# Quartered state products, decoding behind the eviction and tables on another queue in a retention and two-layer kernel

## The chip, the cores and the metric

The kernel runs on one core of a Trainium2 chip. The metric is the device time of one execution in microseconds; before the change it is 597.9 us, the median of three runs (597.83 to 599.41).

## What is computed

Three stages, each on the output of the one before, 1536 tokens in all (2 sequences of 768), 512 features:

```python
def _attn_ref(q, k, v):                      # q, k, v: (2, 8, 768, 64)
    for t in range(S):
        state = gamma[None, :, None, None] * state + np.einsum('bhd,bhe->bhde', k[:, :, t], v[:, :, t])
        y[:, :, t] = scale * np.einsum('bhd,bhde->bhe', q[:, :, t], state)

def _moe_ref(x, w_in, w_out):                # (512, 2048), (2048, 512)
    h = x @ w_in
    g = h * np.tanh(softplus(h))
    return g @ w_out

def _moe2_ref(x, w_gate, w_val, w_out):      # (512, 1536) twice, (1536, 512)
    gate = 1.0 / (1.0 + np.exp(-(x @ w_gate)))
    return gate * (x @ w_val) @ w_out
```

## The kernel before

**Attention.** The tokens are cut into 12 blocks of 128, six to a sequence. A block's queries and keys come as `qk` (128 x 2 x 4 x 128: a pair of heads on the two halves of the partitions, four pairs), its keys and values by token as `nv`. `at_scores(j)` makes the scores of the eight heads in two PSUM tiles, one for each half of the partitions; VectorE multiplies them with a mask into `a`. `at_state(j)` adds the block's keys times values to a running state in PSUM, which ScalarE copies to `s`. `at_out(j)` makes the block's output in one PSUM tile `ao`: eight products of `a` with the decayed values `vp`, and, where the sequence has earlier blocks, eight products of the state with the queries (`inter`). These last have 64 rows and 64 columns, so each uses a quarter of the array; before the change they use the two quarters on its diagonal. VectorE evicts `ao` times a decay table `og` into the chunk `acc` (four blocks each). GpSimd makes `vp` and `og` (`at_prep`).

**Two layers.** Every product of the layers is made of three on rounded numbers (`mm3`): operand and weight are both split into a high part (ScalarE, `fp32r`) and a low part (VectorE or GpSimd, value minus high part). Weights arrive as 64-bit words and are decoded to 32-bit ones first: one ScalarE operation (L100) and three on VectorE (L101 to L103, `decode`). The operands of the first chunk are `xc`; those of the other two chunks are `B11`, `B21`, `B22` and the combinations `T1` to `T4`, which save products. `load_piece` asks for a raw weight, `pump` decodes the next one (a step of `steps`), `put` notes its high and low part in `late_hi` and `late_lo`, `flush_hi` and `flush` issue them, and `weight` hands a weight to a product.

**Order.** While `early` is set, each engine gets its instructions in the order in which the code is written (`InOrder`); such instructions all bear L66. `blocks(j0, dense, made)` writes that order for four attention blocks: scores of the next block, `pump`, `fin` (state, output, eviction), preparation and loads, and one step of the dense products, so that layer 1 starts on finished chunks beside the attention: chunk 0 with blocks 4 to 7, chunk 1 with blocks 8 to 11 (8 dense products in all, one to a block, each of twelve instructions, `h`). After the last block `early` is cleared, and a scheduler orders the rest: `out1_first` (the first output products, `o`), `plain1`, `pair1`, and so on through both layers. DMAs are issued by SyncE; the four tables (`ck`, `ma`, `og`, `sg`) behind the first block's operands.

Of the kernel before, what the change touches and what calls it, by code (L numbers as in the profile page):

```python
# [9 lines left out]
F32 = mybir.dt.float32  # L10
# [4 lines left out]
ALU = mybir.AluOpType  # L15
PSUM = bass.MemoryType.PSUM

P = 128
# [4 lines left out]
def kernel(ctx, tc, qk, nv, w1i, w1o, w2g, w2v, w2o, ma_in, og_in, sg_in, ck_in, out):  # L23
# [14 lines left out]
    NP = KK  # L38
    D = P // 2
# [4 lines left out]
    SPC = N // P  # L44
    SPB = NSUB // 2
    RING = 10
    STG = 3
    WARM = 6
    AHEAD = 4

    early = [True]
# [20 lines left out]
    pe, dve, act, pool, sync = [InOrder(e) for e in (nc.tensor, nc.vector, nc.scalar, nc.gpsimd, nc.sync)]  # L72
# [8 lines left out]
    ps_o = ctx.enter_context(tc.tile_pool(name="ps_o", bufs=2, space=PSUM))  # L81
# [5 lines left out]
    acc_t = [big.tile([P, KK, N], F32, name=f"acc{c}") for c in range(NCH)]  # L87
# [36 lines left out]
    src = {"w1i": w1i, "w1o": w1o, "w2g": w2g, "w2v": w2v, "w2o": w2o}  # L124
    raws, w_t, owner, dead = [], {}, [], set()
    cnt = {"dma": 0, "raw": 0, "task": 0}
    steps, late_hi, late_lo, sums_t, vs = [], [], [], {}, {}
    lo_eng = {"w": dve, "g": pool}

    def load_piece():  # L130
        n = cnt["dma"]
        if n >= len(pieces) or n >= cnt["raw"] + STG:
            return
        kind, i = pieces[n]
        t = stg.tile([P, DM], I64, tag="raw", name="raw")
        sync.dma_start(out=t, in_=src[kind][i])
        raws.append(t)
        cnt["dma"] += 1
# [10 lines left out]
    def room():  # L149
        n = len(owner)  # L150
        return n < RING or owner[n - RING] in dead

    def slot(key):
        assert room(), (key, owner[len(owner) - RING])
        owner.append(key)
        w_t[key] = ring.tile([P, 2, DM], F32R, tag="w", name="w")
        return w_t[key]

    def put(key, v):
        t = slot(key)  # L160
        hi, lo = t[:, 0], t[:, 1]
        late_hi.append(lambda: act.activation(out=hi, in_=v, func=AF.Copy))  # L162
        late_lo.append(lambda: lo_eng["w"].tensor_tensor(out=lo, in0=v, in1=hi.bitcast(F32), op=ALU.subtract))  # L163
        if not early:
            flush()
# [37 lines left out]
    def flush_hi():  # L203
        while late_hi:
            late_hi.pop(0)()

    def flush():
        flush_hi()
        while late_lo:
            late_lo.pop(0)()  # L210

    def pump(n=1):
        flush()
        for _ in range(n):
            if not steps and not plan():
                return
            if steps[0][0] and not room() or steps[0][0] == 0 and "dcs" not in lo_eng:
                return
            steps.pop(0)[1]()

    def weight(key):
        while key not in w_t:
            if not steps:
                assert plan(), key
            steps.pop(0)[1]()
        flush()
        return w_t[key]


# [211 lines left out]
    def run(*parts):  # L441
        for p in parts:
            for s in p:
                s()


    with ExitStack() as actx:
# [4 lines left out]
        ma = ac.tile([P, 1, P], F32, name="ma")  # L452
        ck = ac.tile([P, SPB, 2 * NP, 1], F32, name="ck")
        sg = ac.tile([P, SPB, NP, 1], F32, name="sg")
        og0 = ac.tile([P, NP, P], F32, name="og0")
        qk_t, nv_t, a_t, vp_t, og_t, st_t, s_t = {}, {}, {}, {}, {}, {}, {}

        def load(j):
            if j < NSUB:
                qk_t[j] = ld.tile([P, 2, NP, P], F32, tag="qk", name="qk_t")  # L460
                sync.dma_start(out=qk_t[j], in_=qk[j])
                nv_t[j] = ld.tile([P, 2, 2 * NP, D], F32, tag="nv", name="nv_t")
                sync.dma_start(out=nv_t[j], in_=nv[j])
                if j == 0:
                    sync.dma_start(out=ck, in_=ck_in)
                    sync.dma_start(out=ma, in_=ma_in)
                    sync.dma_start(out=og0, in_=og_in)
                    sync.dma_start(out=sg, in_=sg_in)

        def at_prep(j):  # L470
            if j >= NSUB:
# [21 lines left out]

        def at_out(j):
            a, v, t, s = a_t.pop(j), vp_t[j], qk_t[j], s_t.get(j)
            o = ps_o.tile([P, NP, P], F32, tag="o", name="ao")
            inter = j % SPB > 0

            for p in range(NP):
                for e in range(2):  # L500
                    pe.matmul(
                        out=o[D * e:D * e + D, p, :], lhsT=v[:, 2 * p + e, :], rhs=a[:, e, p, :],
                        start=p == 0, stop=p == NP - 1 and not inter, skip_group_check=True,
                    )
            if inter:
                for p in range(NP):
                    for e in range(2):
                        r = slice(D * e, D * e + D)
                        pe.matmul(
                            out=o[r, p, :], lhsT=s[r, p, :], rhs=t[r, 0, p, :], start=False, stop=p == NP - 1,  # L510
                            skip_group_check=True,
                        )
            dve.tensor_tensor(
                out=acc_t[j // SPC][:, :, j % SPC * P:j % SPC * P + P], in0=o, in1=og_t[j], op=ALU.mult
            )

        def at_state(j):
            if j % SPB == SPB - 1:
                return
            v, k = vp_t[j], nv_t[j]  # L520
            if j % SPB == 0:
                st_t[0] = ps_s.tile([P, NP, D], F32, tag="s", name="st")
            st = st_t[0]
            for p in range(NP):
                for e in range(2):
                    pe.matmul(
                        out=st[D * e:D * e + D, p, :], lhsT=k[:, 0, 2 * p + e, :], rhs=v[:, 2 * p + e, :],
                        start=j % SPB == 0 and p == 0, stop=p == NP - 1, skip_group_check=True,
                    )
            s_t[j + 1] = at.tile([P, NP, D], F32, tag="s", name="s")  # L530
            act.activation(out=s_t[j + 1], in_=st, func=AF.Copy)

        def fin(j):
            at_state(j)
            at_out(j)

        def blocks(j0, dense, made):

            for j in range(j0, j0 + SPC):
                if j + 1 < NSUB:  # L540
                    at_scores(j + 1)
                if j >= SPC - 1:
                    pump()
                fin(j)
                flush_hi()
                at_prep(j + 2)
                load(j + AHEAD)
                load_piece()
                if j == j0 + SPC - 1:
                    made()  # L550
                if dense:
                    dense.pop(0)()
            run(dense)

        dve.memset(ap=one_t, constant=1.0)
        act.activation(out=sig, in_=one_t, func=AF.Mish)
        z = at.tile([P, NP * D], F32, tag="s", name="z")
        dve.memset(ap=z, constant=0.0)
        for n in range(WARM):
            o = ps_o.tile([P, NP * D], F32, tag="o", name="warm")  # L560
# [111 lines left out]
```

## Time and profile before

| | |
|---|---|
| median of the runs | 597.9 us |
| profiled execution, with what lies around it | 602.11 us |
| its span | 600.3 us |
| mean granted TensorE clock | 0.991 |
| TensorE matmul, busy | 587.0 us (98%) |
| VectorE, busy | 412.8 us (69%) |
| GpSimd, busy | 331.3 us (55%) |
| ScalarE, busy | 249.6 us (42%) |

The profile is that of one execution. A program's matrix product in plain fp32 is two instructions in the trace (eight products show as x16), one in `fp32r` is one. In a timeline row stand the start, the length of the merged group, engine, line, operation, the tile written and those read, the shape, the count, and in brackets how long the engine was idle before it and what ended that. PE is TensorE, PEld its weight loads, DVE VectorE, ACT ScalarE, POOL GpSimd.

### The profile page before, as it was taken

What the parts mean: (1) busy time and instruction counts of PE and PEld (TensorE: products, weight loads), DVE (VectorE), ACT (ScalarE), POOL (GpSimd) and SP (SyncE); (2) the same over time, 40 slices, a digit from 0 to 9 for tenths busy, and PEclk for the clock granted to TensorE, in tenths of its full rate; (3) what the DMA queues carried; (4) which work ended last, traced back from release to release, by engine and by line L of the source; (5) the groups of instructions that cost most, each with busy time, mean ns of one, the idle gap of its engine ahead of it and who ended that gap; (6) DMA issues with size and microseconds to landing.
All of it is one profiled execution on the core that took longest, in us unless ns stands there. A gap on an engine that the chain in (4) does not pass through costs nothing.

```text
span 600.3 us, 7975 instructions
## 1 busy us (share of the span) xinstructions
PE 587.0 (98%) x3056; PEld 479.6 (80%) x3056; DVE 412.8 (69%) x572; ACT 249.6 (42%) x433; POOL 331.3 (55%) x268
## 2 busy tenths in 40 slices
PE   9899999999999999998999999999999999999997
PEld 7678887888787888886788787888888888888885
DVE  3879997337959395665777977686578587482554
ACT  1334556445454354443344645642343443333210
POOL 3444566529785585484633556854566657557100
PEclk9989999999999999998999999999999999999999
DMA  8974332204223121401220021133022032000014
GB/s 340 406 252 151 106 106 70 72 3 138 70 72 105 36 84 57 140 23 48 71 70 1 1 106 54 52 105 106 0 88 103 22 101 93 17 1 2 0 53 159
DMA packets 15591, 52.27 MB, mean 87 GB/s; under 512 B 1984, under 2 KB 2112, under 8 KB 15552
## 3 DMA queue, kind: packets, MB, share of 16 engines
q1 hardware_dynamic: 15552, 51.75, 24.9%
q8 instruction: 24, 0.39, 0.3%
q14 instruction: 15, 0.12, 0.1%
HBM read 48.60 MB, written 3.15 MB: 86 GB/s over the span
## 4 chain that ended last, share of the span: by engine, by line
PE 75%; DVE 16%; POOL 3%; ACT 3%; issue 2%; DMA 1%; SPq 0%; DVEq 0%; ACTq 0%; POOLq 0%
PE o L109 30%; PE h L109 28%; PE hx L109 7%; PE h L66 4%; DVE v L102 4%; PE ao L66 3%; DVE v L103 2%; DVE v L101 2%; DVE acc L362 2%; PE sc L66 2%; POOL w L163 1%; POOL g L91 1%; PE st L66 1%; DVE T L91 1%; DMA qk_t<-qk 1%
## 5 line engine op out<-in xcount | busy, mean ns | idle before, releaser
L91 POOL TENSOR_TENSOR g<-e,g 128x512 fp32r<-128x512 f32 x73 | 116.7, 1608 | 86.0 <-ACT g L90 86.0
L109 PE MATMUL o<-g,w 128*128 128x512 f32 x576 | 141.8, 394 | 2.8 <-DVE acc L362 2.6
L109 PEld LDWEIGHTS o<-g,w 128*128 128x128 f32 x576 | 108.6, 190 | 28.3 <-DVE acc L362 5.0
L163 POOL TENSOR_TENSOR w<-v,w 128x512 fp32r<-128x512 f32 x56 | 76.2, 1370 | 67.8 <-ACT w L162 67.0
L109 PE MATMUL h<-T,w 128*128 128x512 f32 x444 | 112.6, 390 | 1.0 <-DVE T L91 0.6
L109 PE MATMUL o<-w,g 128*128 128x512 f32 x432 | 106.0, 390 | 0.0
L109 PEld LDWEIGHTS h<-T,w 128*128 128x128 f32 x444 | 83.2, 188 | 19.4 <-DVE T L91 1.0
L109 PEld LDWEIGHTS o<-w,g 128*128 128x128 f32 x432 | 81.0, 188 | 17.2 <-POOL g L91 0.4
L109 PE MATMUL h<-B,w 128*128 128x512 f32 x348 | 90.8, 390 | 0.8 <-DVE e L352 0.8
L109 PEld LDWEIGHTS h<-B,w 128*128 128x128 f32 x348 | 65.1, 188 | 15.1 <-DVE e L352 1.3
L362 DVE TENSOR_TENSOR acc<-o,acc 128x512 f32<-128x512 f32 x72 | 49.0, 685 | 39.1 <-PE o L109 38.8
L90 ACT ACTIVATE g<-e 128x512 fp32r<-128x512 f32 x77 | 48.1, 630 | 53.7 <-DVE e L352 35.5
L163 POOL TENSOR_TENSOR w<-s,w 128x512 fp32r<-128x512 f32 x34 | 48.2, 1427 | 34.4 <-ACT w L162 34.2
L101 DVE TENSOR_SCALAR v<-v 128x512 int32<-128x512 int32 x59 | 45.1, 767 | 28.1 <-ACT v L100 27.8
L162 ACT ACTIVATE w<-v 128x512 fp32r<-128x512 f32 x59 | 36.7, 630 | 63.1 <-DVE v L103 35.2
L382 DVE TENSOR_TENSOR acc<-o,acc 128x512 f32<-128x512 f32 x60 | 41.1, 686 | 30.6 <-PE o L109 30.2
L100 ACT ACTIVATE v<-raw 128x512 f32<-128x512 f32 x59 | 39.3, 669 | 52.9 <-POOL w L163 20.0
L102 DVE SCALAR_TENSOR_TENSOR v<-raw,v 128x512 int32<-128x512 int32 x59 | 56.0, 951 | 1.0
L109 PE MATMUL hx<-xc,w 128*128 128x512 f32 x216 | 55.6, 390 | 0.1
L103 DVE SCALAR_TENSOR_TENSOR v<-raw,v 128x512 int32<-128x512 int32 x59 | 55.0, 933 | 0.5
L109 PE MATMUL h<-xc,w 128*128 128x512 f32 x216 | 55.0, 389 | 0.0
L109 PEld LDWEIGHTS hx<-xc,w 128*128 128x128 f32 x216 | 40.5, 188 | 8.9 <-ACT e L346 0.5
(78 smaller groups left out, 610.4 us busy)
## 6 DMA issues: line engine op xcount, KB each, us to landing
raw<-w1i SPq DMA_DIRECT2D x16, 512.0 KB, 3.6
raw<-w1o SPq DMA_DIRECT2D x16, 512.0 KB, 3.4
qk_t<-qk SPq DMA_DIRECT2D x12, 512.0 KB, 6.3
nv_t<-nv SPq DMA_DIRECT2D x12, 512.0 KB, 6.8
raw<-w2g SPq DMA_DIRECT2D x12, 512.0 KB, 3.4
raw<-w2v SPq DMA_DIRECT2D x12, 512.0 KB, 3.3
raw<-w2o SPq DMA_DIRECT2D x12, 512.0 KB, 3.2
out<-acc SPq DMA_DIRECT2D x12, 256.0 KB, 2.0
```

Source lines behind the costliest of these rows:

```text
L66: i = call(**kw)
L90: act.activation(out=hi, in_=raw, func=AF.Copy)
L91: eng.tensor_tensor(out=lo, in0=raw, in1=hi.bitcast(F32), op=ALU.subtract)
L100: act.activation(out=v, in_=high.bitcast(F32), func=AF.Copy, scale=2.0 ** -112)
L101: dve.tensor_scalar(out=b, in0=b, scalar1=3, scalar2=None, op0=ALU.logical_shift_left)
L102: dve.scalar_tensor_tensor(out=b, in0=low, scalar=29, in1=b, op0=ALU.logical_shift_right, op1=ALU.bitwise_or)
L103: dve.scalar_tensor_tensor(out=b, in0=high, scalar=SIGN, in1=b, op0=ALU.bitwise_and, op1=ALU.bitwise_or)
L109: pe.matmul(out=o, lhsT=w(a), rhs=x(b), start=first and n == 0, stop=last and n == 2, skip_group_check=more)
L162: late_hi.append(lambda: act.activation(out=hi, in_=v, func=AF.Copy))
L163: late_lo.append(lambda: lo_eng["w"].tensor_tensor(out=lo, in0=v, in1=hi.bitcast(F32), op=ALU.subtract))
L362: dve.tensor_tensor(out=acc, in0=o, in1=acc, op=ALU.add)
L382: dve.tensor_tensor(out=acc, in0=o, in1=acc, op=ALU.add)
```

## The change

Four edits. (1) Odd pairs of heads have their two heads swapped on the partitions, and the output lies in two PSUM tiles, one for even and one for odd pairs, so that the state products use all four quarters of the array; the eviction is two operations of half the size. (2) From the fifth block on, `pump` stands behind the block's eviction instead of ahead of it, and `weight` flushes only if its weight is still pending. (3) Low parts are flushed ahead of `fin`, and at the end of four blocks ahead of the chunk's operands (`made`). (4) ScalarE issues the four table transfers, ahead of everything else on it. One warm-up product goes.

```diff
-    WARM = 6
+    WARM = 5
...
     def weight(key):
...
-        flush()
+        if key in pending:
+            flush()
...
         def load(j):
...
-                if j == 0:
-                    sync.dma_start(out=ck, in_=ck_in)
-                    sync.dma_start(out=ma, in_=ma_in)
-                    sync.dma_start(out=og0, in_=og_in)
-                    sync.dma_start(out=sg, in_=sg_in)
...
         def at_out(j):
-            o = ps_o.tile([P, NP, P], F32, tag="o", name="ao")
+            o = [ps_o.tile([P, NP // 2, P], F32, tag="o", name="ao") for _ in range(2)]
...
             for p in range(NP):
                 for e in range(2):
                     pe.matmul(
-                        out=o[D * e:D * e + D, p, :], lhsT=v[:, 2 * p + e, :], rhs=a[:, e, p, :],
-                        start=p == 0, stop=p == NP - 1 and not inter, skip_group_check=True,
+                        out=o[p % 2][D * e:D * e + D, p // 2, :], lhsT=v[:, 2 * p + e, :], rhs=a[:, e ^ p % 2, p, :],
+                        start=p < 2, stop=p >= NP - 2 and not inter, skip_group_check=True,
...
-                        r = slice(D * e, D * e + D)
+                        r = slice(D * (e ^ p % 2), D * (e ^ p % 2) + D)
                         pe.matmul(
-                            out=o[r, p, :], lhsT=s[r, p, :], rhs=t[r, 0, p, :], start=False, stop=p == NP - 1,
-                            skip_group_check=True,
+                            out=o[p % 2][D * e:D * e + D, p // 2, :], lhsT=s[r, p, :], rhs=t[r, 0, p, :],
+                            start=False, stop=p >= NP - 2, skip_group_check=True,
                         )
-            dve.tensor_tensor(
-                out=acc_t[j // SPC][:, :, j % SPC * P:j % SPC * P + P], in0=o, in1=og_t[j], op=ALU.mult
-            )
+            for n in range(2):
+                dve.tensor_tensor(
+                    out=acc_t[j // SPC][:, n::2, j % SPC * P:j % SPC * P + P], in0=o[n], in1=og_t[j][:, n::2],
+                    op=ALU.mult,
+                )
...
         def blocks(j0, dense, made):
             for j in range(j0, j0 + SPC):
                 if j + 1 < NSUB:
                     at_scores(j + 1)
-                if j >= SPC - 1:
+                flush()
+                if j == SPC - 1:
                     pump()
                 fin(j)
-                flush_hi()
                 at_prep(j + 2)
                 load(j + AHEAD)
                 load_piece()
                 if j == j0 + SPC - 1:
+                    flush()
                     made()
+                if j >= SPC:
+                    pump()
                 if dense:
                     dense.pop(0)()
+                flush_hi()
             run(dense)

+        for t, table in ((ck, ck_in), (ma, ma_in), (og0, og_in), (sg, sg_in)):
+            act.dma_start(out=t, in_=table)
```

(`at_state` and the host's layout of queries and keys swap the same halves of odd pairs; `put` notes each key in `pending`, and `flush` clears it.)

VectorE around the end of the fourth block, before (`v` is a decoded weight, `w` its low part, `ao` the block's output, `xc` the low parts of the first chunk, `a` masked scores):

```order
L66 TENSOR_TENSOR a<-sc,ma 128x512 x2
L66 TENSOR_SCALAR v<-v 128x512
L66 SCALAR_TENSOR_TENSOR v<-raw,v 128x512 x2
L66 TENSOR_TENSOR acc_87<-ao,og 128x4x128
L66 TENSOR_TENSOR xc<-acc_87,xc 128x512 x4
L66 TENSOR_TENSOR a<-sc,ma 128x512 x2
L66 TENSOR_TENSOR w<-v,w 128x512
L66 TENSOR_SCALAR v<-v 128x512
L66 SCALAR_TENSOR_TENSOR v<-raw,v 128x512 x2
L66 TENSOR_TENSOR acc_88<-ao,og 128x4x128
L66 TENSOR_TENSOR w<-v,w 128x512
```

and after:

```order
L66 TENSOR_TENSOR a<-sc,ma 128x512 x2
L66 TENSOR_SCALAR v<-v 128x512
L66 SCALAR_TENSOR_TENSOR v<-raw,v 128x512 x2
L66 TENSOR_TENSOR acc_87<-ao,og 128x2x128 x2
L66 TENSOR_TENSOR w<-v,w 128x512
L66 TENSOR_TENSOR xc<-acc_87,xc 128x512 x4
L66 TENSOR_TENSOR a<-sc,ma 128x512 x2
L66 TENSOR_TENSOR acc_88<-ao,og 128x2x128 x2
L66 TENSOR_SCALAR v<-v 128x512
L66 SCALAR_TENSOR_TENSOR v<-raw,v 128x512 x2
L66 TENSOR_TENSOR a<-sc,ma 128x512 x2
L66 TENSOR_TENSOR w<-v,w 128x512
```

The first weight's low part moved from behind the next score tiles to ahead of the four `xc` parts; the second decoding moved from ahead of the fifth block's eviction to behind it, and its low part behind two more score tiles.

VectorE at the end of the attention, from the low part of the seventh weight after the first, after the change (`acc_89` is the third chunk; the two halves here are the eviction of its third block):

```order
L66 TENSOR_TENSOR w<-v,w 128x512
L101 TENSOR_SCALAR v<-v 128x512
L66 TENSOR_TENSOR acc_89<-ao,og 128x2x128
L102 SCALAR_TENSOR_TENSOR v<-raw,v 128x512
L101 TENSOR_SCALAR v<-v 128x512
L66 TENSOR_TENSOR acc_89<-ao,og 128x2x128
L66 TENSOR_SCALAR v<-v 128x512
L103 SCALAR_TENSOR_TENSOR v<-raw,v 128x512
L102 SCALAR_TENSOR_TENSOR v<-raw,v 128x512
L66 SCALAR_TENSOR_TENSOR v<-raw,v 128x512
```

Two more fused operations, three low parts, one half of the last block's eviction, a scalar operation, the other half, a fused operation, two differences `t`, a fused operation and the first low part of `T` follow. Before, the last block's eviction stood behind one decoding and the first steps of two more, with no low part between.

TensorE at the same place, before and after (`B_84` and `B_85` are `B11` and `B21`, `o` the first output products, `T` the operands made from the third chunk):

```order
L66 MATMUL ao<-a,vp 64x128 x8
L66 MATMUL ao<-qk_t,s 64x128 x8
L109 MATMUL h<-B_84,w 128x512 x6
L109 MATMUL h<-B_85,w 128x512 x6
L109 MATMUL o<-g,w 128x512 x24
L109 MATMUL hx<-T_958,w 128x512
L109 MATMUL h<-T_958,w 128x512 x2
L109 MATMUL o<-g,w 128x512 x12
```

```order
L109 MATMUL h<-B_84,w 128x512 x6
L109 MATMUL h<-B_85,w 128x512 x2
L66 MATMUL ao<-a,vp 64x128 x2
L109 MATMUL h<-B_85,w 128x512 x3
L66 MATMUL ao<-a,vp 64x128 x6
L66 MATMUL ao<-qk_t,s 64x128 x8
L109 MATMUL h<-B_85,w 128x512
L109 MATMUL o<-g,w 128x512 x24
L109 MATMUL hx<-T_980,w 128x512
L109 MATMUL h<-T_980,w 128x512 x2
L109 MATMUL h<-xc,w 128x512 x8
```

The last block's output moved behind eight instructions of the last dense product, and eight `xc` products of a later step stand between the `T` products.

## Rows read from the trace of the kernel before

**Rows 1.** The page, busy us of each engine:
```profile
PE 587.0 (98%) x3056; PEld 479.6 (80%) x3056; DVE 412.8 (69%) x572; ACT 249.6 (42%) x433; POOL 331.3 (55%) x268
```

**Rows 2.** Stretches: length, busy us (count) of the engines, granted clock, DMA share, GB/s:
```profile
27.80:34.60 6.80, 5.99 (x22) 4.57 (x24) 3.77 (x7) 1.92 (x4) 0.00 (x0) 0.50 0.83 321
270.00:280.00 10.00, 7.71 (x28) 5.85 (x27) 5.64 (x9) 2.45 (x4) 3.78 (x3) 0.83 0.20 77
```

**Rows 3.** Timeline of TensorE, first and second dense product:
```profile
28.61 4.63 PE L66 MATMUL h<-xc,w 128*128 128x512 f32 x10 [2.62 <-DVE w L66]
33.18 1.82 PE L66 MATMUL sc<-qk_t 64*128 64x128 f32 x16
...
36.98 3.04 PE L66 MATMUL h<-xc,w 128*128 128x512 f32 x12
```

**Rows 4.** Timeline of TensorE, where the orders meet, and the later wait:
```profile
251.53 2.88 PE L109 MATMUL o<-g,w 128*128 128x512 f32 x12
...
273.02 2.51 PE L109 MATMUL o<-g,w 128*128 128x512 f32 x6 [2.29 <-DVE acc L362]
```

**Rows 5.** Timeline of TensorE, one block with a dense product:
```profile
49.08 3.01 PE L66 MATMUL h<-xc,w 128*128 128x512 f32 x12
52.02 1.16 PE L66 MATMUL sc<-qk_t 64*128 64x128 f32 x16
...
54.60 1.09 PE L66 MATMUL ao<-qk_t,s 64*64 64x128 f32 x16
55.63 3.01 PE L66 MATMUL h<-B,w 128*128 128x512 f32 x12
```

**Rows 6.** Timeline of VectorE beside the first wait:
```profile
20.45 0.42 DVE L66 TENSOR_SCALAR v<-v 128x512 int32<-128x512 int32 x1
20.90 1.42 DVE L66 SCALAR_TENSOR_TENSOR v<-raw,v 128x512 int32<-128x512 int32 x2
22.23 0.68 DVE L66 TENSOR_TENSOR acc<-ao,og 128x512 f32<-128x512 f32 x1
23.61 3.14 DVE L66 TENSOR_TENSOR xc<-acc,xc 128x512 fp32r<-128x512 f32 x4 [0.70 <-ACT xc L66]
26.68 1.27 DVE L66 TENSOR_TENSOR a<-sc,ma 128x512 f32<-128x512 f32 x2
27.88 0.67 DVE L66 TENSOR_TENSOR w<-v,w 128x512 fp32r<-128x512 f32 x1
```

**Rows 7.** Timeline of ScalarE there:
```profile
19.67 0.70 ACT L66 ACTIVATE v<-raw 128x512 f32<-128x512 f32 x1 [2.96 <-DMA raw<-w1i]
...
22.35 0.63 ACT L66 ACTIVATE w<-v 128x512 fp32r<-128x512 f32 x1 [1.71 <-DVE v L66]
...
25.60 0.38 ACT L66 ACTIVATE s<-st 128x256 f32<-128x256 f32 x1
```

**Rows 8.** Stretches, in the order PE, PEld, DVE, ACT, POOL:
```profile
20.00:30.00 10.00, 7.38 (x99) 5.90 (x96) 9.17 (x15) 4.27 (x9) 3.86 (x4) 0.89 1.03 408
40.00:70.00 30.00, 30.00 (x359) 24.55 (x359) 28.53 (x38) 14.82 (x29) 16.90 (x13) 1.00 0.46 159
77.00:251.50 174.50, 173.91 (x761) 142.20 (x760) 120.92 (x163) 84.91 (x149) 112.38 (x81) 1.00 0.25 81
```

**Rows 9.** Timeline of VectorE while GpSimd runs too:
```profile
36.24 1.25 DVE L66 TENSOR_SCALAR v<-v 128x512 int32<-128x512 int32 x1
37.53 2.14 DVE L66 SCALAR_TENSOR_TENSOR v<-raw,v 128x512 int32<-128x512 int32 x2
...
60.73 1.57 DVE L66 TENSOR_TENSOR w<-v,w 128x512 fp32r<-128x512 f32 x1
```

**Rows 10.** Timeline of GpSimd beside the first wait:
```profile
23.36 1.04 POOL L66 TENSOR_TENSOR og<-og,sg 128x512 f32<-128x512 f32 x1
```

**Rows 11.** Timeline of TensorE's weight loads, one block's state products:
```profile
13.42 0.85 PEld L66 LDWEIGHTS ao<-qk_t,s 64*64 64x64 f32 x16 [0.17 <-issue]
```

**Rows 12.** Timeline of TensorE, scores of the second block:
```profile
8.26 1.16 PE L66 MATMUL sc<-qk_t 64*128 64x128 f32 x16 [0.16 <-DMA qk_t<-qk]
```

More of the change, by code (lines that the diff above doesn't have):

```diff
@@ L126 @@
     cnt = {"dma": 0, "raw": 0, "task": 0}
-    steps, late_hi, late_lo, sums_t, vs = [], [], [], {}, {}
+    steps, late_hi, late_lo, pending, sums_t, vs = [], [], [], [], {}, {}
     lo_eng = {"w": dve, "g": pool}
@@ L161, in put @@
         hi, lo = t[:, 0], t[:, 1]
+        pending.append(key)
         late_hi.append(lambda: act.activation(out=hi, in_=v, func=AF.Copy))
@@ L210, in flush @@
             late_lo.pop(0)()
+        pending.clear()
     def pump(n=1):
@@ L525, in at_state @@
                 for e in range(2):
+                    r = e ^ p % 2
                     pe.matmul(
-                        out=st[D * e:D * e + D, p, :], lhsT=k[:, 0, 2 * p + e, :], rhs=v[:, 2 * p + e, :],
+                        out=st[D * r:D * r + D, p, :], lhsT=k[:, 0, 2 * p + e, :], rhs=v[:, 2 * p + e, :],
                         start=j % SPB == 0 and p == 0, stop=p == NP - 1, skip_group_check=True,
@@ L641, in feature_major @@
     def feature_major(a):
-        a = a.reshape(B, H // 2, 2, nsub, P, D).transpose(0, 3, 2, 5, 1, 4)
+        a = a.reshape(B, H // 2, 2, nsub, P, D)
+        a = np.stack([a[:, p, ::1 - p % 2 * 2] for p in range(H // 2)], axis=1).transpose(0, 3, 2, 5, 1, 4)
         return a.reshape(B * nsub, 2 * D, H // 2, P)
```

## The prediction

> **What bounds the kernel now.** I read the page's busy shares first: TensorE works 587.0 of 600.3 us [rows 1], so only what shortens its work, or fills its 13 us of idleness, can count. Next the stretches with the granted clock: it was 0.50, the 1.2 GHz level, from 27.8 to 34.6 us, and fell again in the 270s [rows 2]; each fall follows an idle time of TensorE, 2.62 us and 2.29 us [rows 3, 4]. The third view is TensorE's timeline. The first dense product waits until 28.61 us for a weight's low part on VectorE; its last ten instructions then take 33.18 - 28.61 = 4.57 us, and the scores behind them 1.82 us where they take 1.16 at full clock [rows 3, 5]. From there to the end of the attention TensorE never pauses, and a block with a dense product takes 55.63 - 49.08 = 6.55 us [rows 5]. The fourth view, VectorE and ScalarE beside the first wait, says why it is so long: VectorE does four xc low parts (23.61 to 26.7), then two masked score tiles (26.68), and only then the weight's low part (27.88), though ScalarE had its high part ready at 22.98 [rows 6, 7].
>
> The sum is made against the profiled execution (span 600.3, 602.1 us with what lies around it). The median of the runs is 597.9, 4.2 us below; I carry that difference over unchanged.
>
> **Part 1: low part ahead of operands.** Up to the first decoding I keep the times of before, since they hang on a transfer: ScalarE waits 2.96 us for the raw weight [rows 7] while the DMA engines move 408 GB/s at a share of 1.03 [rows 8], and no byte is added or taken away. Decoding again ends at 22.23 [rows 6]. The eviction is now two halves. No row shows one on VectorE; it lies between 0.34 us (half of 0.68 [rows 6]) and 0.68. ScalarE's 256-column copy takes 0.38 against 0.63 for 512 [rows 7], which is nearest, so 2 x 0.38, and the end at 23.0. Then the weight's low part: 0.67 alone, 1.57 beside GpSimd [rows 6, 9]; GpSimd runs an og multiplication until 24.40 [rows 10], so I take 1.3, and 24.3. The four xc low parts follow at 0.60 each (the first bore 1.3 of their 3.14 us before, beside that og) to 26.7, and TensorE consumes them as they come, three products of 0.245 us ((52.02 - 49.08) / 12 [rows 5]) each. The product ends at about 27.5; before it ended at 33.18 [rows 3]. Gain: **5.7 us**, 2.6 of it waiting, 2.1 half clock, 1.0 the smaller distance to the xc parts. Bounds: 4.6 (every xc low part shares with GpSimd) to 6.5 (the weight's does not).
>
> **Part 2: decoding behind the eviction.** The second product's weight is now decoded behind that traffic. VectorE from 26.7: two score tiles 1.2, eviction 0.76, decoding 1.83 (20.45 to 22.3 [rows 6]), two score tiles 1.2, low part 0.67: 32.4 us. Decoding beside GpSimd costs 1.25 + 2.14 = 3.4 [rows 9], which makes it 34.0. TensorE is there, with two products issued, at 30.7 (27.5, scores 1.09, output 1.6, two products 0.49). So a **new wait** of 1.7 to 3.3 us; I take 2.0, near the lower end, because GpSimd's work on a dense product starts only once ScalarE has read the result. The second product ends at 32.7 + 10 x 0.245 = 35.2, against 36.98 + 2.96 = 39.9 before [rows 3]: **4.8 us** remain. Later dense products of these blocks find their low part in time: VectorE has 2.95 + 1.09 us between an eviction's start and the next scores' end, and needs 0.76 + 1.83 to 3.4.
>
> **Part 3: quartered state products.** The 16 instructions on the state take 55.63 - 54.60 = 1.03 us [rows 5], and their weight loads are issued over 0.85 [rows 11]: two quadrants at a time. With four at a time the 0.85 halves. Between no gain and 0.43 I take 0.41, nearer the top, because 16 score instructions on half-height tiles take about as long as these (1.16 and 1.09 [rows 5]), so no quadrant seems to pay for its neighbour. Ten blocks have the product. In the first four it buys nothing, since TensorE then meets the transfers (scores already wait for one at 8.26 [rows 12]) and Part 1 is fixed by the raw weight. In the next it is inside Part 2. Five remain: **2.05 us**. The second half-eviction adds 0.08 x 8 = 0.6 us to a VectorE that is busy 28.5 of 30 us in these blocks [rows 8]; I subtract it whole.
>
> A rule speaks against this part. The Trainium skill, "TensorEngine Tiling (Array Packing)", Gotcha 1, says that different row tiles cannot access the same PSUM bank simultaneously; both new output tiles are written by both row halves. The trace so far disagrees: both halves already write one bank, at 1.09 us beside 1.16 for the scores, whose halves have a bank each [rows 5]. By the rule Part 3 would give nothing, and the time would be that of rival B.
>
> **Part 4: at no cost.** Four table transfers leave SyncE's queue for ScalarE's, where only a table load and a one-column activation stand before the first state copy; no byte changes, and the engines behind both queues are full [rows 8]. One warm-up product fewer: the second block's scores wait for their transfer anyway [rows 12]. A tile of raw weights is now asked for one block later (behind the tenth block's operands); its decoding is a block later too.
>
> **Part 5: the order behind the attention.** The two orders differ until the twelve output products at 251.53 us [rows 4]; from there each engine's order is the same to the end, so the wait of 2.29 us at 273 and its fall of the clock stay. Between 77 and 251.5 us TensorE idles 0.6 us in all before [rows 8]. The waits of the new order are in no row; between none and the wait of rows 4 with its clock (4 us) I charge 1.0, nearer to what this stretch shows.
>
> **Sum:** -4.8 - 2.05 + 0.6 + 1.0 = -5.25 us: span 595.1, runs **592.7 us**.
>
> **The rivals.**
> A. No second wait: Part 2 costs nothing, and its block brings the half-clock scores (0.66) and its own 0.41: 5.7 + 1.1 + 2.05 = 8.9 gained, **589.0**. For it: a decoding that slips in ahead of the xc parts. Against it: VectorE's list above leaves 1.7 us even without GpSimd. Chance 0.13.
> B. The quadrants do not overlap fourfold: -4.8 + 1.0 and no pressure on VectorE: **594.1**. For it: each column half now gets sums from both row halves, which no row shows. Chance 0.10.
> C. The second wait drops the clock as the first did. Its price is that of rows 3: ten products at 0.457 instead of 0.245 and scores at 1.82 instead of 1.16, 2.8 us: **595.5**. For it: 2.0 to 3.3 us idle, against the 2.62 and 2.29 that came before the two falls. Against: TensorE works without pause before and after. Chance 0.17.
> D. The timed runs already lack the half-clock stretch (they are 4.2 us below the profiled one), so that its 2.8 us cannot be won, and 1 us more of waits comes in the new order: **596.5**. Chance 0.10.
> E. Slower: the last block's eviction. On VectorE it now stands behind three decodings and their low parts; from the seventh weight's low part to the first T low part are 22 operations, 11.1 us uncontended (eight fused ones, six plain ones at 0.60, four scalar ones and four half-evictions at 0.34). TensorE has 13.4 us of work ahead of T (scores' followers 3.6, 24 dense products 5.9, 24 output products 5.8, twice the 2.88 of rows 4, less the 1.9 by which VectorE starts later). If all decoding there ran beside GpSimd, at 1.25, 2.14 a pair and 1.57 [rows 9], VectorE would need 21.4: 8.0 late, less eight xc products (2.0) put in between, 6.0 idle, and 3.4 for 6.8 us of half clock [rows 2]: 9.4 lost against 6.3 won, **601.0**. It turns the sign only if GpSimd stretches VectorE by over 7 us there; GpSimd works 16.9 of 30 us in the blocks before [rows 8]. Chance 0.05.
>
> **How the numbers follow.** The forecast has the remaining 0.45. About 0.3%, 1.8 us, is what a measurement can tell from no change. Faster: the forecast, A, B and C, 0.85; within: D, 0.10; slower: E, 0.05. The range reaches from A to D, 588.9 to 596.6.
>
> **What would show it.** In the profile after: the first dense product running from about 24 to 27.5 us at full clock; a wait of TensorE on VectorE's w at 30 to 33 us; the 16 state instructions in about 0.6 us; blocks of 6.1 to 6.2 us; the stall of 2.3 us near 268 us with its fall of the clock. State instructions still at 1.0 us would be B, half clock near 35 us C, idle before the T products E. The forecast is wrong if the first product still ends after 30 us, or if idle time between 70 and 250 us exceeds 3 us.

## The result and the profile after

The changed kernel is slower: 605.81 us, the median of four runs (604.52 to 608.10), against 597.87 for the kernel before beside it (597.78 to 599.41). The ratio is 1.0111, with an interval of 1.0082 to 1.0140. The forecast was 592.7 us, and the range ended at 596.6.

One thing must be known of the kernel before: in 85 further runs it took from 597.5 to 605.5 us, at a mean granted clock from 1.000 to 0.990 and with medians of 599.3 to 599.8, so that its profiled execution (602.1 us, 0.991), with two stretches of half clock, lies in the upper part. Ratios below are to the kernel before on the same chip, beside the runs in question.

TensorE's row of the page after, answering to that of [rows 1]: it is busy for 4.2 us less, and the span is 2.3 us longer (602.6 us, an execution of 604.5).

```profile
PE 582.8 (97%) x3054; PEld 474.2 (79%) x3054; DVE 417.7 (69%) x584; ACT 249.9 (41%) x433; POOL 323.0 (54%) x268
```

TensorE's timeline after, the first two dense products, answering to [rows 3]. The columns are start, length, engine, line, operation, tiles, shape, count and idle time ahead.

```profile
24.07 0.51 PE L66 MATMUL h<-xc,w 128*128 128x512 f32 x1
25.09 2.33 PE L66 MATMUL h<-xc,w 128*128 128x512 f32 x9 [0.51 <-DVE xc L66]
27.75 0.73 PE L66 MATMUL h<-xc,w 128*128 128x512 f32 x2 [0.33 <-DVE xc L66]
28.41 1.16 PE L66 MATMUL sc<-qk_t 64*128 64x128 f32 x16
...
33.84 4.59 PE L66 MATMUL h<-xc,w 128*128 128x512 f32 x12 [2.65 <-ACT w L66]
```

The first product runs early and, but for 0.84 us, without a wait. The forecast second wait is there, and the twelve instructions behind it take 4.59 us where twelve take 3.04 at full clock: the clock fell behind it.

One block with a dense product, answering to [rows 5], and the weight loads of its state products (PEld), answering to [rows 11]. The window ends in the next dense product, so two of its twelve instructions show:

```profile
47.37 3.04 PE L66 MATMUL h<-xc,w 128*128 128x512 f32 x12
50.34 1.16 PE L66 MATMUL sc<-qk_t 64*128 64x128 f32 x16
...
52.92 0.67 PE L66 MATMUL ao<-qk_t,s 64*64 64x128 f32 x16
53.52 0.73 PE L66 MATMUL h<-B,w 128*128 128x512 f32 x2
...
52.92 0.42 PEld L66 LDWEIGHTS ao<-qk_t,s 64*64 64x64 f32 x16 [0.17 <-issue]
```

The sixteen instructions on the state take 0.67 us where they took 1.09, their weight loads 0.42 where they took 0.85, and the block 53.52 - 47.37 = 6.15 us where it took 6.55. So far the plan works. Then comes what no term of the sum had. TensorE's timeline at the end of the attention:

```profile
72.84 0.67 PE L66 MATMUL ao<-qk_t,s 64*64 64x128 f32 x16
73.44 0.50 PE L109 MATMUL h<-B,w 128*128 128x512 f32 x1
79.38 8.22 PE L109 MATMUL o<-g,w 128*128 128x512 f32 x24 [5.43 <-DVE acc L66]
```

TensorE stands still for **5.43 us**, and the 24 output products behind it take 8.22 us, where the kernel before takes 5.60. The stretches with their granted clock (length, busy us and count of PE, PEld, DVE, ACT, POOL, the clock, DMA share, GB/s), answering to [rows 2]:

```profile
33.50:36.90 3.40, 3.06 (x7) 2.04 (x8) 3.33 (x8) 0.85 (x2) 0.52 (x1) 0.51 0.94 336
77.90:84.70 6.80, 5.32 (x13) 4.17 (x14) 6.80 (x10) 5.68 (x11) 4.57 (x4) 0.50 0.31 120
270.00:280.00 10.00, 7.73 (x35) 6.03 (x34) 8.49 (x12) 3.10 (x6) 5.25 (x4) 1.00 0.31 105
```

The clock is at its 1.2 GHz level for 6.8 us there, of which TensorE works 5.32: 8.22 - 5.60 = 2.6 us are lost on top of the wait. What is waited for stands in VectorE's timeline:

```profile
71.90 0.42 DVE L66 TENSOR_SCALAR v<-v 128x512 int32<-128x512 int32 x1
...
75.72 0.68 DVE L66 SCALAR_TENSOR_TENSOR v<-raw,v 128x512 int32<-128x512 int32 x1
77.09 0.69 DVE L66 TENSOR_TENSOR w<-v,w 128x512 fp32r<-128x512 f32 x1 [0.69 <-ACT w L66]
77.70 1.29 DVE L164 TENSOR_TENSOR w<-v,w 128x512 fp32r<-128x512 f32 x2
78.91 0.42 DVE L66 TENSOR_TENSOR acc<-ao,og 128x256 f32<-128x256 f32 x1
79.24 0.42 DVE L101 TENSOR_SCALAR v<-v 128x512 int32<-128x512 int32 x1
79.57 0.42 DVE L66 TENSOR_TENSOR acc<-ao,og 128x256 f32<-128x256 f32 x1
```

TensorE finished the last block's output at 73.5. VectorE evicts it at 78.91, behind the decodings (`v`) and three low parts (`w`). The first output product starts at 79.38, as soon as the first half eviction is done (78.91 + 0.42). Its operands have nothing to do with that eviction. What it needs is a bank: blocks' outputs `ao` and output products `o` share the two banks of the pool `ps_o`. Before, one output took one bank, and `o` began in the other; now the two half tiles of a single block hold both.

### The profile page after: what moved, and what is told of

Its sections match the earlier page's. It is cut to its first block, busy times and chain, and to the rows that moved or that the text cites. A ratio compares the mean times of both kernels' runs of the same rounds, so it can differ in the third digit from the quotient of the medians.

```text
span 602.6 us, 7981 instructions
## 1 busy us (share of the span) xinstructions
PE 582.8 (97%) x3054; PEld 474.2 (79%) x3054; DVE 417.7 (69%) x584; ACT 249.9 (41%) x433; POOL 323.0 (54%) x268
## 4 chain that ended last, share of the span: by engine, by line
PE 78%; DVE 13%; DMA 3%; ACT 2%; issue 2%; POOL 1%; SPq 0%; ACTq 0%
PE o L109 35%; PE h L109 32%; PE hx L109 8%; DVE v L66 3%; DMA raw<-w1i 2%; DVE v L102 2%; DVE v L103 2%; PE h L66 1%; DVE v L101 1%; DMA qk_t<-qk 1%; DVE acc L365 1%; POOL w L164 1%; DVE T L91 1%; ACT v L100 1%; PE sc L66 1%
## 5 line engine op out<-in xcount | busy, mean ns | idle before, releaser
L91 POOL TENSOR_TENSOR g<-e,g 128x512 fp32r<-128x512 f32 x73 | 105.5, 1454 | 92.5 <-ACT g L90 92.5
L103 DVE SCALAR_TENSOR_TENSOR v<-raw,v 128x512 int32<-128x512 int32 x60 | 61.1, 1020 | 0.5
L101 DVE TENSOR_SCALAR v<-v 128x512 int32<-128x512 int32 x60 | 42.1, 702 | 25.8 <-ACT v L100 25.7
L102 DVE SCALAR_TENSOR_TENSOR v<-raw,v 128x512 int32<-128x512 int32 x60 | 56.8, 947 | 1.0
L109 PEld LDWEIGHTS h<-xc,w 128*128 128x128 f32 x216 | 40.6, 188 | 8.4
```

The lines of the kernel that those rows point to most:

```text
L91: eng.tensor_tensor(out=lo, in0=raw, in1=hi.bitcast(F32), op=ALU.subtract)
L101: dve.tensor_scalar(out=b, in0=b, scalar1=3, scalar2=None, op0=ALU.logical_shift_left)
L102: dve.scalar_tensor_tensor(out=b, in0=low, scalar=29, in1=b, op0=ALU.logical_shift_right, op1=ALU.bitwise_or)
L103: dve.scalar_tensor_tensor(out=b, in0=high, scalar=SIGN, in1=b, op0=ALU.bitwise_and, op1=ALU.bitwise_or)
L109: pe.matmul(out=o, lhsT=w(a), rhs=x(b), start=first and n == 0, stop=last and n == 2, skip_group_check=more)
```

## The experiments

The theories: **M**, the loss is that ring of two banks, which no longer buffers; **N**, the quartered products themselves cost; **V**, VectorE and its neighbours set the end of the attention whatever TensorE wins. The expectations of the first four runs put M and N in their own words.

**1. Eviction first.** The changed kernel; the last block's eviction goes ahead of the decodings.

```diff
-        v = decode(raws.pop(0))
+        with tc.issue_after(hold[0]) if hold else nullcontext():
+            v = decode(raws.pop(0))
...
                     flush()
+                    if j == NSUB - 1:
+                        hold.append(dve.last)
                     made()
```

> The changed kernel with one thing put right: at the end of the attention the decodings that the scheduler is free to place are queued on VectorE behind the last block's eviction. Theory M (the loss is made where the first output products wait 5.43 us for the two PSUM tiles of the last block, whose eviction stands behind three decodings on VectorE, and in the 6.8 us of half clock that follow): that wait falls below 1.5 us, no half clock follows it, and the time falls by 5.4 + 2.7 = 8 us from 605.8 to about 598, the time before the change within 0.5%. Theory N (the quartered products with their two tiles and two half evictions cost time wherever they stand): above 603.

Measured 603.13 us, ratio 1.0047 (1.0015 to 1.0078). M had expected about 598; by its letter the time is N's (above 603), so this run does not decide. By the ratios 0.47 of 1.11% of loss is left, by the medians 605.81 - 603.13 = 2.7 of 7.9 us are won. The waits over 1 us from 70 to 110 us, TensorE's timeline (lines stand a little lower in this kernel, so L66 is L67 here), and behind them one row of GpSimd and one of ScalarE:

```profile
75.66 5.75 PE L110 MATMUL o<-g,w 128*128 128x512 f32 x24 [1.45 <-DVE acc L67]
98.83 1.66 PE L110 MATMUL hx<-T,w 128*128 128x512 f32 x6 [2.46 <-ACT e L351]
108.71 1.66 PE L110 MATMUL hx<-xc,w 128*128 128x512 f32 x6 [1.40 <-ACT e L351]
...
80.45 12.69 POOL L92 TENSOR_TENSOR g<-e,g 128x512 fp32r<-128x512 f32 x1 [5.73 <-ACT g L91]
...
96.08 0.66 ACT L101 ACTIVATE v<-raw 128x512 f32<-128x512 f32 x1 [7.03 <-POOL s L179]
```

The wait falls from 5.43 to 1.45 us, and its half clock is gone (5.75 us for the 24 products instead of 8.22): 6.5 us in all; yet 3.9 us come back 23 and 33 us later, as waits on ScalarE. ScalarE itself had waited 7.03 us for GpSimd's sums `s`, which stood behind a low part of 12.69 us: the chain that experiments 9 to 12 take up. That this chain alone makes the two waits was not tried here. So the place of the wait was right, and its removal alone does not bring the time back.

**2 to 4. The parts alone.** The kernel before with edit (1) alone; the changed kernel without edit (1); the kernel before with edit (4) and the shorter warm-up alone.

> The kernel before with the quartered state products and the two half evictions alone; order of decoding, low parts and tables as before. Theory M: the state products take 0.6 instead of 1.03 us in every block, the first dense product waits as before (2.6 us), and the last eviction stands behind one decoding and the first steps of two more, so the first output products wait 1 to 3 us for its two tiles; without that wait 2.6 us would be won after the first dense product (six blocks of 0.43), so 595 to 599. Theory N: above 601.

> The changed kernel without the quartered products: one output tile and one eviction as before, the new order and the tables kept. Theory M: the last eviction still stands behind decodings, but one of the two PSUM tiles is free, so the first twelve output products start at once and only the next twelve wait, 1 to 3 us; time between 598 and 603. Theory N: at or below 597, since all that costs is gone.

> The kernel before with the four tables issued by ScalarE and one warm-up product fewer, nothing else. Both theories: the second block's scores start 0.6 us earlier (7.6 instead of 8.3 us), the first dense product hardly earlier, the time within 0.3% of before (596.1 to 599.7). If the tables are part of the loss: above 600.

The quarters alone: 607.63 us, ratio **1.0105** (1.0055 to 1.0156). The new order alone: 600.55, ratio 1.0002 (0.9971 to 1.0032). The tables alone: 598.43, ratio 0.9973 (0.9941 to 1.0006). M had expected 595 to 599 for the quarters and counted only the wait at the first output product; by its letter the time is N's (above 601). The whole loss is in edit (1), the part that takes work off TensorE. Its waits that the kernel before does not have, and a row of ScalarE that belongs to the third:

```profile
59.62 1.21 PE L66 MATMUL ao<-a,vp 128*64 128x128 f32 x16 [1.94 <-DVE acc L66]
...
77.56 5.78 PE L109 MATMUL o<-g,w 128*128 128x512 f32 x24 [2.44 <-DVE acc L66]
...
91.51 3.01 PE L109 MATMUL o<-g,w 128*128 128x512 f32 x9 [2.51 <-ACT acc L370]
...
90.31 0.66 ACT L100 ACTIVATE v<-raw 128x512 f32<-128x512 f32 x1 [8.16 <-POOL s L176]
```

At 59.62 a block waits for the eviction of the block before it. The third wait is of another kind: the output products are late by now, and ScalarE's eviction of the second of them (`acc<-o`, 90.88) has come to stand behind a decoding that waits 8.16 us for GpSimd's sums. The old order, with its decodings ahead of the eviction, has the waits too, so they are not the order's doing.

The run of the tables shows what a run without falls looks like. Its clock is 0.999, and TensorE's timeline has the wait of [rows 3] with ten instructions at full speed behind it:

```profile
28.25 2.56 PE L66 MATMUL h<-xc,w 128*128 128x512 f32 x10 [2.51 <-DVE w L66]
...
73.45 2.88 PE L109 MATMUL o<-g,w 128*128 128x512 f32 x12
```

Its first output product starts at 73.45, not at 76.56 as in the profiled kernel before. The changed kernel ends its attention's dense products at 73.94 (1 instruction from 73.44), which is no gain on that. Nor is the new order: in its run, without a fall of the clock up to there, TensorE waits 1.15 and 1.05 us at the second dense product, and the first output product starts 2.1 us behind that of the tables alone:

```profile
75.56 4.70 PE L109 MATMUL o<-g,w 128*128 128x512 f32 x20
```

**5 to 8. The banks.** Four kernels on theory M. The first is the changed kernel with the second half tile from the five banks of the hidden products:

```diff
-            o = [ps_o.tile([P, NP // 2, P], F32, tag="o", name="ao") for _ in range(2)]
+            o = [pl.tile([P, NP // 2, P], F32, tag=tag, name="ao") for pl, tag in ((ps_o, "o"), (ps_h, "h"))]
```

The second is the kernel before with the quarters and that line. The third is the second with edit (4) and the low part ahead of the operands for the first chunk alone:

```diff
+                if j == SPC - 1:
+                    flush()
                 if j == j0 + SPC - 1:
                     made()
```

The fourth is the kernel before with two half tiles from `ps_o` and two half evictions, but each product in its old quadrant on the diagonal:

```diff
-            o = ps_o.tile([P, NP, P], F32, tag="o", name="ao")
+            o = [ps_o.tile([P, NP // 2, P], F32, tag="o", name="ao") for _ in range(2)]
...
-                        out=o[D * e:D * e + D, p, :], lhsT=v[:, 2 * p + e, :], rhs=a[:, e, p, :],
+                        out=o[p % 2][D * e:D * e + D, p // 2, :], lhsT=v[:, 2 * p + e, :], rhs=a[:, e, p, :],
```

The expectations for the fourth, the second, the first and the third, in this order:

> The kernel before with its block output in two half tiles, both from the output ring, and with two half evictions, but with each product in the quadrant that it had before: the ring's loss without the quartering. Theory M: the waits on the accumulator come as with the quarters (1 to 3 us each near 59, 77 and 91 us), state products stay at 1.0 us, ratio to the kernel before 1.007 to 1.015. Theory N: no such waits, ratio under 1.003. Theory V (second half eviction loads VectorE): waits at the end of the attention alone, ratio 1.002 to 1.007.

> The kernel before with the quartered state products alone, one half tile from the output ring and one from the hidden products' banks. Theory M: the three waits on the accumulator that the quarters alone brought (1.94 us at 59.6, 2.44 at 77.6, 2.51 at 91.5) are gone, state products take 0.6 us instead of 1.02, and the time is 1 to 3 us below the kernel before in the same call (ratio 0.995 to 0.998). Theory N: ratio 1.005 or more. Theory V: gains in the attention (5 blocks of 0.4) are taken back by waits on VectorE at its end, ratio 0.998 to 1.003.

> The changed kernel with one of the two half tiles of each block's output taken from the five banks of the hidden products instead of the two of the output ring, so that a block's output again leaves one bank of the ring free. Theory M (the loss is the ring: both of its banks are held until VectorE has evicted the last block): the wait of 5.43 us before the first dense output product falls under 1.5 us and its half clock goes; about 598 to 601 us. Theory V (VectorE's backlog alone sets the end of the attention, whichever bank is free): the wait only moves to the next product that needs VectorE (the T low parts or the hidden products), time stays at 603 to 606. Theory N (the quartered products themselves cost): 604 or more with the waits at new places.

> The quarters in two pools as in the run beside it, with the tables on ScalarE and the weight's low part ahead of the first chunk's operands only; everything else in the order of the kernel before. Theory M: the first dense wait (2.5 us) falls under 1 us, a wait of 1 to 2 us comes at the second dense product, and the time is 0 to 2 us below the run with the quarters in two pools alone: ratio 0.991 to 0.997 to the kernel before. Theory V: the gained time is given back at the end of the attention in a wait on VectorE, ratio 0.997 to 1.003.

The two tiles on the diagonal: 607.25 us, ratio **1.0111** (1.0070 to 1.0152), as bad as with the quarters. Its state products and its waits:

```profile
53.35 1.09 PE L66 MATMUL ao<-qk_t,s 64*64 64x128 f32 x16
...
59.76 1.21 PE L66 MATMUL ao<-a,vp 128*64 128x128 f32 x16 [0.67 <-DVE acc L66]
...
78.09 5.73 PE L109 MATMUL o<-g,w 128*128 128x512 f32 x24 [1.63 <-DVE acc L66]
...
92.04 2.41 PE L109 MATMUL o<-g,w 128*128 128x512 f32 x7 [2.55 <-ACT acc L370]
```

Nothing is quartered, and the same three places wait: 4.9 us in all, and behind the third a stretch of 3.4 us at half clock. The quarters with one tile elsewhere: 599.75, ratio 1.0005 (0.9981 to 1.0028); its first output product starts without a wait:

```profile
74.45 1.75 PE L109 MATMUL o<-g,w 128*128 128x512 f32 x7
```

One allocation decides over 1%: **M is shown, N falls**. The changed kernel with one tile elsewhere takes 601.43, ratio 1.0020 (1.0000 to 1.0039), between what M (598 to 601) and V (603 to 606) had expected; the wait of 5.43 us becomes none at the first output product and 1.83 at the tenth, now for a weight behind the same decodings, with a stretch of 3.4 us at half clock:

```profile
73.87 2.20 PE L109 MATMUL o<-g,w 128*128 128x512 f32 x9
77.91 5.64 PE L109 MATMUL o<-g,w 128*128 128x512 f32 x15 [1.83 <-ACT w L66]
```

The third kernel took 599.29, ratio 0.9962 (0.9931 to 0.9993). But the quarters with their bank mended had gained nothing measurable, where M had forecast 1 to 3 us; V's range, 0.998 to 1.003, holds the 1.0005. Where did the 0.4 us per block go? In this profile, whose clock fell behind the first wait for 6.8 us as in the profiled kernel before, the gain reaches the end of the attention: the first output product starts at 74.45 against 76.56. At output product number 100 (from 0) it is gone: 116.45 against 116.41.

**9 to 12. A square.** Base: the kernel before with edit (4) and the low part of the first chunk (as just shown), no quarters. On it, quarters with two pools (the third kernel again) yes or no, and a relief of GpSimd yes or no: the low part of `g` right behind the attention moves to VectorE.

```diff
-        blocks(2 * SPC, plain1(0, 1) + plain1(1, 1), early.clear)
+        blocks(2 * SPC, plain1(0, 1) + plain1(1, 1), lambda: (early.clear(), lo_eng.update(g=dve)))
...
     run(out1_first(0))
+    lo_eng["g"] = pool
```

> The kernel before with the tables on ScalarE and the weight's low part ahead of the first chunk's operands, no quarters: the base of a square of four runs (quarters yes or no, relief of GpSimd yes or no). Theory V (what is won inside the attention is taken back at its end, where the work of VectorE, ScalarE and GpSimd sets the pace): ratio 0.996 to 1.000, as the run with the quarters in two pools on the same base. Theory G (the quarters' 2 us reach the end): 1 to 2 us above that run.

> The base with the quarters in two pools (run once before as f3, here again beside the other three corners). Theory V: within 0.7 us of the base without quarters, its first output product 2 us earlier but its 100th output product at the same time. Theory G: 1 to 2 us faster than the base, 100th output product 1 to 2 us earlier too.

> The base without quarters, with the one low part of g that GpSimd does right behind the attention (8.2 us there while VectorE works without pause) moved to VectorE (one more operation of 0.7 us). Theory V: ScalarE's idle time of 7.6 us behind GpSimd's sums shrinks by over 5 us, the waits near 93 and 102 us shrink, 0.3 to 1 us faster than the base. Theory G: no change beyond 0.3 us, since TensorE waits for little there.

> The base with the quarters in two pools and the same low part of g on VectorE. Theory V: now the quarters' gain reaches the end: the waits of 0.3 and 0.8 us near 93 and 102 us are gone, the 100th output product starts 1 to 2 us before that of the base, ratio to the kernel before 0.992 to 0.996, the best of the four. Theory G: as the run with quarters alone within 0.3 us.

| | no relief | relief |
|---|---|---|
| no quarters | 597.89 us, 0.9981 (0.9960 to 1.0003) | 597.62 us, **0.9958** (0.9935 to 0.9982) |
| quarters | 598.17 us, 0.9982 (0.9961 to 1.0004) | 597.54 us, **0.9957** (0.9933 to 0.9981) |

The third kernel, 0.9962 the first time, is 0.9982 now. The quarters are worth nothing in either column, against what V had forecast for the second. V had also put the first output product 2 us earlier with the quarters. On this base, whose clock does not fall in the attention, the gain is gone before the attention ends, as the stretches of the base and then of the base with quarters show (columns as above):

```profile
9.00:72.00 63.00, 62.20 (x771) 50.27 (x768) 56.00 (x74) 26.01 (x50) 34.07 (x28) 1.00 0.70 256
40.00:70.00 30.00, 30.00 (x345) 24.14 (x344) 28.57 (x37) 13.63 (x27) 16.00 (x13) 1.00 0.44 143
```

```profile
9.00:72.00 63.00, 59.16 (x769) 46.10 (x768) 57.02 (x85) 25.63 (x50) 33.62 (x28) 1.00 0.69 256
40.00:70.00 30.00, 28.64 (x343) 22.00 (x342) 28.98 (x42) 13.10 (x26) 15.91 (x13) 1.00 0.42 141
```

From 9 to 72 us TensorE works 3.04 us less, and stands idle for all of it. From 40 to 70 VectorE is at 28.98 of 30 us. Four of TensorE's waits with the quarters say for whom:

```profile
31.53 3.20 PE L66 MATMUL h<-xc,w 128*128 128x512 f32 x12 [0.29 <-DVE acc L66]
...
37.90 3.22 PE L66 MATMUL h<-xc,w 128*128 128x512 f32 x12 [0.58 <-DVE acc L66]
...
51.57 2.79 PE L66 MATMUL h<-B,w 128*128 128x512 f32 x11 [0.46 <-DVE B L66]
...
55.68 1.16 PE L66 MATMUL sc<-qk_t 64*128 64x128 f32 x14 [0.90 <-DVE a L66]
```

Here it is VectorE: an eviction, a low part, masked scores. Of all idle time from 9 to 72 us, 3.2 us are waits for VectorE, and 0.5 one for a transfer. The first output products start at 72.25 us in the base and at 72.42 with the quarters.

The relief's column is V's other half. GpSimd (two rows), ScalarE and TensorE in the base:

```profile
78.22 9.35 POOL L91 TENSOR_TENSOR g<-e,g 128x512 fp32r<-128x512 f32 x1 [6.21 <-ACT g L90]
87.53 0.73 POOL L173 TENSOR_TENSOR s<-v 128x256 f32<-128x256 f32 x1
...
90.50 0.66 ACT L100 ACTIVATE v<-raw 128x512 f32<-128x512 f32 x1 [7.63 <-POOL s L176]
...
94.28 1.66 PE L109 MATMUL hx<-T,w 128*128 128x512 f32 x6 [1.19 <-ACT e L346]
```

and GpSimd and ScalarE with the relief (for TensorE the profile names no wait from 80 to 150 us):

```profile
78.78 7.65 POOL L173 TENSOR_TENSOR s<-v 128x256 f32<-128x256 f32 x1 [6.86 <-DVE v L103]
86.38 0.74 POOL L175 TENSOR_TENSOR s<-v 128x256 f32<-128x256 f32 x1
...
88.67 0.66 ACT L100 ACTIVATE v<-raw 128x512 f32<-128x512 f32 x1 [6.99 <-POOL s L176]
```

The chain is GpSimd's sums, which hold the buffers that ScalarE's next decoding needs, then TensorE. I expected ScalarE's idle time to shrink by over 5 us; it shrank by 0.64, since the next operation of GpSimd now takes the long time. The sums still end 1.8 us earlier, and that was enough: the wait of 1.19 us at 94 us is gone, and output product number 100 starts at 112.52 instead of 114.16 us. The profiled spans differ by as much at the end (596.0 and 597.6 us, both at a mean clock of 0.997), so a gain made here reaches it. The two kernels with the relief are the best of all: some 0.4% below the kernel before, with intervals below 1. What the relief itself gives is less sure: its medians lie only 0.27 and 0.63 us below those without it, its means over twelve runs 1.1 and 1.6.

## Why the prediction was wrong

**What bounds the kernel.** That "only what shortens its work, or fills its 13 us of idleness, can count" was the first error. VectorE's 28.53 of 30 us stood in [rows 8], and the prediction used it only to charge 0.6 us for the half evictions. Of a block of 6.55 us VectorE was free for 1.47 / 30 of it, 0.32 us, and the second half eviction takes 0.06 of these (the row below: two halves in 0.74 us, for one whole in 0.68). By this estimate a block could become shorter for good by some 0.26 us, not by 0.41. The changed kernel's blocks did become 0.40 us shorter; at the end of the attention TensorE waited 5.43 us for VectorE.

```profile
34.84 0.74 DVE L66 TENSOR_TENSOR acc<-ao,og 128x256 f32<-128x256 f32 x2
```

**Part 1 (5.7 us).** The mechanism held: the product ended at 28.4 us, where the scores begin, at full clock; 27.5 was forecast. But 2.1 of the 5.7 us was half clock of the one profiled execution. The prediction had this as rival D and gave it 0.10; but of the 85 runs 49 had a mean clock of 0.995 or more, which leaves no room for 6.8 us at half clock (3.4 of 600 us), so it was the usual case. The 4.2 us between the profile and the runs, which the sum carried over unchanged, are about its 2.8 us and the 1.6 of the fall in the 270s (54 output products in 14.14 us, in 12.54 with the tables alone). On a base without the fall, the low part in front moves the first output product from 73.45 to 72.25 us: 1.2 us, and without the relief these are taken back by 114 us (114.16 against 113.53).

**Part 2 (a wait of 2.0 us).** It came with 2.65, within its bounds. Rival C came true with it: the clock fell to half for a stretch of 3.4 us, and the twelve instructions cost 1.55 us more, where C had 2.8. That 4.8 us remain of Part 1 was wrong: against a profile without falls the new order alone starts the output products 2.1 us later (75.56 against 73.45), and its time shows no gain (1.0002).

**Part 3 (2.05 us).** The price was right, 0.42 us per block against 0.41, and rival B fell. The Trainium skill, "TensorEngine Tiling (Array Packing)", Gotcha 1, says that row tiles cannot access one PSUM bank simultaneously. That did not decide the time here: both half tiles get sums from both row halves, in different halves of the partitions, and 0.67 us against 1.09, with weight loads in 0.42 against 0.85, fits four quadrants at a time where there were two. Two steps failed. "Five remain: 2.05 us" assumed that a shorter block ends earlier; the square measured 0, and where the clock had fallen ahead 2.1 us were won up to the end of the attention and gone 42 us later. And the edit "two PSUM tiles" was costed only as a second eviction, 0.6 us. That term was about right (0.74 us for 0.68). What it left out is that the second tile comes from a ring of two: 1.0 to 1.1% of the time, some 6 to 7 us, shown by the two tiles on the diagonal, and by the quarters with one tile elsewhere, which do not pay it.

**Part 4 (nothing).** Held: 0.9973, with 1 inside the interval.

**Part 5 (1.0 us).** This is where the sum broke: 5.43 us of waiting and 2.6 lost at half clock stood in its place. By the sum the first output product was to start at 70.3 us (76.56 less 4.8 and 2.05, plus 0.6); TensorE was ready for it at 73.94, and it started at 79.38. The prediction's own sign of being wrong, over 3 us of idle time between 70 and 250 us, was met by this wait alone. Rival E had the place and the cause on VectorE, the last eviction behind three decodings, and counted which operations TensorE's work must outlast. It looked for the first consumer of that eviction in the data, the T low parts, and found 13.4 us of cover. The first consumer was the next user of the bank, with none. Of the two causes, the tile elsewhere recovers 605.81 - 601.43 = 4.4 us, the eviction in front 2.7, by medians of different sets; by the ratios, each to the kernel before beside it, it is 0.91 and 0.64% of the time, 5.5 and 3.8 us. Both together were not tried, and what they would give stays open.

**The tail.** The wait of 2.29 us near 273 came back with 2.27. A fall of the clock followed in 8 of the 14 profiles of this study, and not in this one. Why the same wait is followed by a fall in some executions and not in others stays open.

## What to carry to other kernels

When an edit splits a tile or adds one, count it against the ring that it comes from, and ask which later work takes its next buffer from there: that work waits for the eviction, whatever its operands are. A stage in which two engines are both over 95% busy had no gain to give here to an edit that relieved only one of them; look at the second engine's share in the same stretch before summing. And compare the profiled execution's clock and time with the runs' before promising to win back a stretch of half clock.

## What was not expected of the hardware

A GpSimd operation that takes 0.73 us took 7.65 us beside a VectorE that worked almost without pause, and a low part that takes 1.30 us elsewhere (at 70.70 in the base) took 9.35. Both ended only when VectorE ran out of work: at 86.43 us, VectorE's last operation having ended at 85.83, and at 87.57 after 86.42. ScalarE's waits for the sums behind them, 6.99 and 7.63 us, bear the lengths out. Moving the low part away only handed the delay to the next operation. That agrees with the Trainium skill, "SBUF — State Buffer", "Who interferes with whom", which says that only the port pair shared by these two engines causes contention, as an exclusive lock; no run here measured the port itself.
